# First-layer activations split for two blocks per instruction, out of a pair of PSUM banks

## The chip, the cores and the metric

The kernel runs on one core of one Trainium2 chip. The metric is the device time of one execution in microseconds (us), as the median over timed runs. A program on one core has one span, that of its instructions; the execution's time is a little longer than the span.

## What is computed

The reference is a depthwise causal convolution over the sequence (7 taps, softmaxed weights, one set for each of 8 heads) and, on its result, a mixture of 8 experts. A greedy pass over all sorted gate logits gives every token to exactly one expert, at most 3584 tokens each; each expert is a two-layer network with 1024 hidden units and no bias.

```python
def _attn_ref(x, weight):                 # x: 8 x 3584 x 192, weight: 8 x 7
    ...
    w = w / (np.sum(w, axis=-1, keepdims=True) + 1e-09)
    ...
    out = np.einsum('hk,bskhg->bshg', w, x_unf)

def _moe_ref(x, w_gate, w1, w2):          # x: 28672 x 192, w1: 8 x 192 x 1024, w2: 8 x 1024 x 192
    ...
    for idx in order:
        tok, e = (int(idx) // E, int(idx) % E)
        if assigned[tok] >= 0 or counts[e] >= cap:
            continue
        assigned[tok] = e
        counts[e] += 1
    ...
    for e in range(E):
        mask = assigned == e
        h = np.maximum(x[mask] @ w1[e], 0.0)
        out[mask] = h @ w2[e]
```

## The kernel before

The program has two stages that overlap a little. For the first 155 us the convolution runs as matmuls with Toeplitz matrices (tiles `cv`), with the gate logits (`pl`, `pt`) behind it. Then comes the expert stage, class `FFN`: 56 tiles of 512 tokens, one after the other, and beside them the rest of the routing (which token goes to which expert), cut into small steps that are strewn between the matmuls.

**A tile of the expert stage.** `FFN.run` (from line 1445) goes over the tiles `i` and in each over 8 steps `f`. One step issues, in this order: `l1(i, f)`, a chance for routing steps (`self.bg()`), a piece of the preparation of tile `i + 1` (`prep`), half of the second layer of tile `i - 1` (`l2`, 8 matmuls, with another `self.bg()` inside), after odd steps the store of a finished output block (`store`), routing again, and a piece of the next expert's weights (`wsplit`). "Tile 3, step 1" below is `i = 3, f = 1`. There is no second layer beside tile 0, as there is no tile before it.

**The first layer.** `l1` (line 1320) computes block `f`: 128 of the 1024 hidden units for 512 tokens. Numbers are kept as a high and a low part, so one block is five matmuls of 512 columns into one PSUM bank `ph`. ScalarE then writes the high part `hh` (a Relu that rounds), and VectorE the low part `hl`, which is max(ph, 0) minus `hh`. `hl` needs `ph` and `hh`; the bank `ph` is free when `hl` is done. `l2` multiplies `hh` and `hl` with the second layer's weights, one tile later.

**PSUM.** Eight banks of 512 fp32 a partition. In the expert stage they are: two for `bg` (pool `bgp`, which all routing matmuls and the last gate logits take in turn), two for `y` (second layer), one for `px` and three for `ph`.

**Preparation.** For tiles 1 to 7 the tokens are transposed on TensorE: `transp` (line 1297) writes four blocks into `px` at step 1 (upper 128 features) and again at step 4 (lower 64). At the next step `evac` takes the high part on ScalarE and the low part on VectorE (`xa`, `xd`). Later tiles are transposed on VectorE or by DMA (`shuffle`, `turn`) and use no `px`. Tile 0 is prepared ahead of the expert stage, in `bg` banks.

**The order of the work.** Each engine executes its own instructions in the order in which the program issues them, and waits on semaphores. Routing steps are issued by a planner: class `Pace` keeps an estimated clock for TensorE, VectorE and ScalarE, to which every instruction adds an estimate by its size (class `Meter`: VectorE 0.15 us plus a term in the number of elements, ScalarE 0.22 us plus such a term). `Steps.hook` issues the next routing step unless VectorE's estimated clock is too far ahead of TensorE's (1.8 us in the expert stage) or ScalarE's (3 us). So what an instruction of `l1` is estimated at also moves the routing steps behind it.

A pool hands out any of its buffers that is free when a tile is asked for. A buffer stays taken until the last instruction that reads its tile, wherever that one stands in the order; the first write of the next tile in it waits for that reader.

Of the kernel before, what the change touches and what calls it, by code (L numbers as in the profile page):

```python
# [6 lines left out]
F32 = mybir.dt.float32  # L7
# [3 lines left out]
AF = mybir.ActivationFunctionType  # L11
OP = mybir.AluOpType
AX = mybir.AxisListType
PSUM = bass.MemoryType.PSUM
# [100 lines left out]
def build(ctx, tc, nc, x, weight, wg, attn, LT, wk):  # L115
# [115 lines left out]
    def logits_t(i):  # L231
# [5 lines left out]
        A.activation(o, v, AF.Copy)  # L237

    k.load, k.conv, k.transp, k.logits, k.logits_t = load, conv, transp, logits, logits_t
    k.toeplitz, k.gate_ops = toeplitz, gate_ops  # L240
    return k
# [909 lines left out]
class FFN:  # L1151
# [145 lines left out]
    def transp(self, i, u, bank=None):  # L1297

        x = self.XG[i]
        p = self.px = bank or self.pt.tile([128, 512], F32, name="px")  # L1300
        for b in range(4):
            q = slice(128 * b, 128 * b + 128)
            if u == 0:
                self.nc.tensor.transpose(p[:, q], x[:, b, 0:128], self.ident)
            else:
                self.nc.tensor.transpose(p[0:64, q], x[:, b, 128:D], self.ident)
        if u:
            self.XG.pop(i)
# [11 lines left out]
    def l1(self, i, key, f):  # L1320
        nc = self.nc
        if f == 0:
            self.H[i] = (self.hp[i % 2].tile([128, 8, 512], FR, name="hh"),
                         self.hp[i % 2].tile([128, 8, 512], FR, name="hl"))
        hh, hl = self.H[i]
        ah, al, dh, dl = self.wt(key)[0:4]
        xa, xd = self.XT[i]
        xh, xl = xa[:, 0], xa[:, 1]
        p = self.ph.tile([128, 512], F32, name="ph")
        s = slice(128 * f, 128 * f + 128)  # L1330
        for n, (wt, xx) in enumerate(((ah, xh), (al, xh), (ah, xl), (dh, xd), (dl, xd))):
            nc.tensor.matmul(p, wt[:, s], xx, start=(n == 0), stop=(n == 4))
            if n == 2:
                self.bg()
        nc.scalar.activation(hh[:, f], p, AF.Relu)
        nc.dve = max(nc.dve, nc.act)
        nc.vector.scalar_tensor_tensor(hl[:, f], p, 0.0, hh[:, f].bitcast(F32), op0=OP.max, op1=OP.subtract)

    def l2(self, i, key, b, half):
        nc = self.nc  # L1340
# [143 lines left out]
def moe_kernel(ctx, tc, x, weight, wg, w1, w2, out):  # L1484
    nc = Pace(tc.nc)
# [5 lines left out]
    with ExitStack() as cw:  # L1491
        pool = lambda c, name, bufs, **kw: c.enter_context(tc.tile_pool(name=name, bufs=bufs, **kw))
        late = dict(reuse_waits="tile")
        right = dict(side="right")
# [5 lines left out]
        r = Route(tc, nc, LT, lst, wk, drm)  # L1500
        r.oh_pool = oh
        r.bg = lambda: bgp.tile([128, 512], F32, name="bg")
        ff = FFN(tc, nc, attn, w1, w2, out, r.ident, wr, drm)
# [140 lines left out]
            k.conv(i, mid)  # L1644
        for c in cx[1], cx[2], cx[3], cc:
            c.close()
        ff.pt = pool(cw, "pt", 1, space=PSUM, **right, **late)
        ff.ph = pool(cw, "ph", 3, space=PSUM, **right, **late)
        bg.drain(3)
        nc.lat, nc.las = (0.8, 1.2)  # L1650
        if not got:
# [81 lines left out]
```

## Time and profile before

| what | value |
|---|---|
| median of 3 timed runs | 1236.66 us (1236.03 to 1237.11) |
| the profiled execution | 1234.62 us |
| its span | 1232.9 us |
| mean granted TensorE clock | 0.998 of full speed |
| first `ph` matmul, last one's start | 155.6 us, 1214.8 us |
| `ph` and `y` matmuls | 2240 and 3584 |
| last `bg` output read | 735.8 us |

The profile is one execution, taken by the hardware profiler. PE is TensorE's matmuls and PEld its weight loads, DVE is VectorE, ACT ScalarE, POOL GpSimd, SP the engine whose queue issues most DMAs. A row of the timeline gives start, duration, engine, line, operation, output and inputs, shapes, count, and in brackets the idle time of that engine just before and what ended it. All arithmetic stands on line 56, a helper, so rows are told apart by the names of their tiles. Matmuls are pipelined: their rows overlap, so the distance of starts is what one costs, not its duration.

### The profile page before, as it was taken

Reading aid. Unit: us, or ns where it says so; the run is one execution under the profiler, and the core shown is the slowest. Engines: PE = TensorE matmul, PEld = TensorE weight load, DVE = VectorE, ACT = ScalarE, POOL = GpSimd, SP = SyncE. Lnnn points to the kernel's source line nnn. Section 1 sums busy time; section 2 is a strip of 40 time slices with the busy share of each in tenths; the row PEclk is TensorE's granted clock in tenths of the full one; section 3 lists DMA queues with packets and bytes.
Section 4 is the critical chain, followed back from the end, with each engine's and each line's share of the span. In section 5 each row is a group of like instructions: output and inputs, shape, how many; then the busy total and the mean of one; then the engine's idle time right before and its main releaser. Section 6 shows DMA issues by size and latency. Waiting matters only on the chain.

```text
span 1232.9 us, 21779 instructions
## 1 busy us (share of the span) xinstructions
PE 1201.0 (97%) x7694; PEld 1034.1 (84%) x7694; DVE 983.1 (80%) x2117; ACT 565.6 (46%) x1252; POOL 540.3 (44%) x528
## 2 busy tenths in 40 slices
PE   4999999999999999999999999999999999999997
PEld 2445678899989988889888889999999999999997
DVE  7398789898998988899979866777777777777762
ACT  4454565556445455454554443333433343334332
POOL 3000344444546555545455435444444544543422
PEclk9999999999999999999999999999999999999999
DMA  9999674659427474655343432114323232423100
GB/s 239 347 344 326 230 223 123 176 158 312 153 59 220 133 246 129 219 159 190 88 132 114 116 106 74 49 40 152 108 91 105 97 107 89 159 72 120 49 24 28
DMA packets 129221, 182.03 MB, mean 148 GB/s; under 512 B 21632, under 2 KB 91728, under 8 KB 127440
## 3 DMA queue, kind: packets, MB, share of 16 engines
q1 hardware_dynamic: 86496, 104.15, 27.3%
q0 software_dynamic: 21504, 44.07, 12.0%
q10 hardware_dynamic: 21104, 32.34, 7.8%
q8 instruction: 62, 1.02, 0.4%
q14 instruction: 55, 0.45, 0.1%
HBM read 102.38 MB, written 78.12 MB: 146 GB/s over the span
## 4 chain that ended last, share of the span: by engine, by line
PE 91%; DVE 4%; DMA 2%; ACT 1%; issue 1%; POOL 0%; SPq 0%; ACTq 0%; POOLq 0%; DVEq 0%
PE ph L56 42%; PE y L56 41%; PE cv L56 3%; PE bg L56 3%; DMA X<-in_x_dram 1%; DVE aT L56 1%; PE pl L56 1%; DMA wgr<-in_moe_w_gate_dram 1%; DVE X L56 1%; PE px L56 0%; ACT a L56 0%; ACT X L56 0%; POOL c_mu L173 0%; SPq L194 0%; DVE hl L56 0%
## 5 line engine op out<-in xcount | busy, mean ns | idle before, releaser
L56 PE MATMUL y<-w,hh 128*128 128x384 f32 x1792 | 535.8, 355 | 0.0
L56 ACT ACTIVATE hh<-ph 128x512 fp32r<-128x512 f32 x448 | 268.0, 598 | 470.8 <-PE ph L56 467.9
L56 PE MATMUL y<-w,hl 128*128 128x192 f32 x1792 | 449.0, 251 | 0.0
L56 DVE SCALAR_TENSOR_TENSOR hl<-ph,hh 128x512 fp32r<-128x512 f32 x448 | 307.9, 687 | 133.3 <-ACT hh L56 127.4
L56 PE MATMUL ph<-xa,w 128*128 128x512 f32 x1344 | 395.0, 402 | 0.0
L56 PEld LDWEIGHTS y<-w,hl 128*128 128x128 f32 x1792 | 340.9, 190 | 16.3
L56 PEld LDWEIGHTS y<-w,hh 128*128 128x128 f32 x1792 | 336.3, 188 | 19.8 <-issue 1.7
L1367 POOL DMA_INDIRECT out_dram<-yo,ia x128 | 145.4, 1136 | 211.5 <-DVE yo L56 180.6
L56 PEld LDWEIGHTS ph<-xa,w 128*128 128x128 f32 x1344 | 218.4, 189 | 20.3 <-issue 1.2
L1367 POOL DMA_INDIRECT out_dram<-yo,ib x96 | 96.0, 1000 | 220.0 <-DVE yo L56 212.6
L56 PE MATMUL ph<-xd,w 128*128 128x512 f32 x448 | 177.7, 397 | 1.2 <-DVE xd L56 1.2
L56 PE MATMUL ph<-xd,dl 128*128 128x512 f32 x448 | 174.2, 389 | 0.3 <-DVE dl L56 0.3
L56 DVE STREAM_TRANSPOSE xs<-xg 32x128 f32<-32x128 f32 (+2 forms) x408 | 164.8, 404 | 6.6
L1292 POOL DMA_INDIRECT xg<-attn,ja x128 | 140.6, 1098 | 46.2 <-issue 40.7
L56 ACT ACTIVATE yt<-y 128x192 f32<-128x192 f32 x224 | 73.2, 327 | 94.3 <-PE y L56 91.7
L56 PE MATMUL cv<-X,TH 118*128 118x384 f32 x256 | 99.5, 517 | 17.3 <-DVE TH L56 12.7
L1292 POOL DMA_INDIRECT xg<-attn,jb x96 | 103.5, 1078 | 29.3 <-issue 29.0
L56 DVE TENSOR_TENSOR yo<-y,yt 128x192 f32<-128x192 f32 x224 | 79.3, 354 | 42.8 <-ACT yt L56 40.2
L56 PEld LDWEIGHTS ph<-xd,w 128*128 128x128 f32 x448 | 84.0, 188 | 21.5 <-DVE xd L56 1.7
L56 PEld LDWEIGHTS ph<-xd,dl 128*128 128x128 f32 x448 | 84.2, 188 | 19.9 <-issue 0.5
L56 PEld LDWEIGHTS cv<-X,TH 118*128 118x128 f32 x256 | 45.1, 195 | 47.7 <-issue 12.5
L56 ACT ACTIVATE a<-cv 128x384 f32<-128x384 f32 x128 | 59.2, 493 | 47.4 <-PE cv L56 23.0
(238 smaller groups left out, 918.0 us busy)
## 6 DMA issues: line engine op xcount, KB each, us to landing
attn<-a ACTq DMA_DIRECT2D x16, 1344.0 KB, 10.2
X<-in_x_dram SPq DMA_DIRECT2D x17, 672.0 KB, 14.3
raw<-in_moe_w_dram SPq DMA_DIRECT2D x56, 192.0 KB, 4.0
X<-in_x_dram ACTq DMA_DIRECT2D x15, 672.0 KB, 10.5
kw<-w SPq DMA_DIRECT2D x36, 256.0 KB, 4.3
kv<-w SPq DMA_DIRECT2D x24, 384.0 KB, 5.7
scr<-xs SPq DMA_DIRECT2D x96, 96.0 KB, 2.6
w<-kw SPq DMA_DIRECT2D x6, 1536.0 KB, 7.2
```

Of the source, the lines that this page charges most:

```text
L56: return f(*a, **k)
L1292: self.nc.gpsimd.indirect_dma_start(out=t[:, b], out_offset=None, in_=self.attn[0:rows], in_offset=bass.IndirectOffsetOnAxis(ap=idx[b], ax ...
L1367: st = self.nc.gpsimd.indirect_dma_start(out=self.out, out_offset=bass.IndirectOffsetOnAxis(ap=idx, axis=0), in_=o, in_offset=None, bounds ...
```

## The change

`l1` takes one `ph` tile of two banks for two neighbouring blocks. It issues nothing on ScalarE and VectorE after an even block; after an odd one a single activation and a single VectorE instruction handle both, 1024 elements a partition each. In the last tile every block is still handled alone. The pool `ph` has two such pairs (four banks) instead of three single banks, and `px` loses its own bank: `transp` takes a `bg` buffer.

```diff
@@ class FFN, transp
-        p = self.px = bank or self.pt.tile([128, 512], F32, name="px")
+        p = self.px = bank or self.bank()
@@ class FFN, l1
-        p = self.ph.tile([128, 512], F32, name="ph")
+        if f % 2 == 0:
+            self.pair = self.ph.tile([128, 2, 512], F32, name="ph")
+        p = self.pair[:, f % 2]
...
-        nc.scalar.activation(hh[:, f], p, AF.Relu)
+        if i == len(self.tiles) - 1:
+            c, p = slice(f, f + 1), self.pair[:, f % 2:f % 2 + 1]
+        elif f % 2:
+            c, p = slice(f - 1, f + 1), self.pair
+        else:
+            return
+        nc.scalar.activation(hh[:, c], p, AF.Relu)
         nc.dve = max(nc.dve, nc.act)
-        nc.vector.scalar_tensor_tensor(hl[:, f], p, 0.0, hh[:, f].bitcast(F32), op0=OP.max, op1=OP.subtract)
+        nc.vector.scalar_tensor_tensor(hl[:, c], p, 0.0, hh[:, c].bitcast(F32), op0=OP.max, op1=OP.subtract)
@@ moe_kernel
-        ff.pt = pool(cw, "pt", 1, space=PSUM, **right, **late)
-        ff.ph = pool(cw, "ph", 3, space=PSUM, **right, **late)
+        ff.bank = r.bg
+        ff.ph = pool(cw, "ph", 2, space=PSUM, **right, **late)
```

The rows below are the instructions in the order in which one engine executes them, with the semaphores that one waits for in brackets; the number behind a tile's name tells tiles of one name apart.

First place: ScalarE in tile 0, steps 1 to 3, before. `bg_1883` holds transposed logits, `bg_1887` the next batch of logits, `px_1869` the transposed tokens of tile 1.

```order
L56 ACTIVATE hh_1818<-ph_1850 128x512 [waits PE_49]
L56 ACTIVATE w2_1845<-raw_1561 128x2x192 [waits DMAHW2_49]
L56 ACTIVATE LT_75<-bg_1883 128x8x16 [waits PE_49]
L56 ACTIVATE hh_1818<-ph_1879 128x512 [waits PE_49]
L56 ACTIVATE xa_1908<-px_1869 128x512
L56 ACTIVATE L_1920<-bg_1887 128x4x16 [waits PE_49]
```

The same place of the changed kernel; the tokens are now in `bg_1863`, the two logit tiles in `bg_1877` and `bg_1881`.

```order
L56 ACTIVATE hh_1815<-ph_1817 128x1024 [waits PE_49,Pool_49]
L56 ACTIVATE w2_1840<-raw_1561 128x2x192 [waits DMAHW2_49]
L56 ACTIVATE LT_75<-bg_1877 128x8x16 [waits PE_49]
L56 ACTIVATE xa_1900<-bg_1863 128x512
L56 ACTIVATE L_1912<-bg_1881 128x4x16 [waits PE_49]
```

What moved: one `hh` of 1024 stands where two of 512 stood, and three tiles of the two-buffer pool are read one after the other. TensorE writes them in the order 1863, 1877, 1881:

```order
L56 MATMUL bg_1863<-ident_79,xg_1577 128x128 [waits DMASW7_49]
L56 MATMUL ph_1873<-xa_1747,w1_1548 128x512 x3
L56 MATMUL bg_1877<-ident_79,L_1856 128x128 [waits PE_49,Activation_49]
L56 MATMUL bg_1881<-aT_1773,c_mu_142 32x128 [waits DVE_49,Activation_49]
L56 MATMUL bg_1881<-aT_1773,c_mu_142 32x128 [waits DVE_49] x3
```

Before, the fourth of these rows named other semaphores:

```order
L56 MATMUL px_1869<-ident_79,xg_1577 128x128 [waits DMASW7_49]
L56 MATMUL ph_1879<-xa_1750,w1_1548 128x512 x3
L56 MATMUL bg_1883<-ident_79,L_1862 128x128 [waits PE_49,Activation_49]
L56 MATMUL bg_1887<-aT_1776,c_mu_142 32x128 [waits DVE_49,PE_49]
L56 MATMUL bg_1887<-aT_1776,c_mu_142 32x128 [waits DVE_49] x3
```

The first write of `bg_1881` now waits for ScalarE too: while `bg_1863` is unread it can only have the buffer of `bg_1877`.

Second place: VectorE in tile 0 from step 3 on, before (`w1`, `w2`, `dl` are weight splits, `M1`, `m_f`, `F` routing).

```order
L56 SCALAR_TENSOR_TENSOR hl_1819<-ph_1927,hh_1818 128x512 [waits Activation_49]
L56 TENSOR_REDUCE M1_76<-LT_75 128x16 [waits Activation_49]
L56 TENSOR_TENSOR w2_1845<-raw_1676,w2_1845 128x2x192 [waits DMAHW5_49,Activation_49]
L56 SCALAR_TENSOR_TENSOR hl_1819<-ph_1955,hh_1818 128x512 [waits Activation_49]
L56 SCALAR_TENSOR_TENSOR m_f_1963<-M1_76,Ts_77 128x128 [waits DVE_49]
L56 TENSOR_TENSOR F_1004<-LT_75,m_f_1963 128x4x128 [waits DVE_49]
L56 TENSOR_TENSOR w1_1971<-raw_1848,w1_1971 128x512 [waits DMAHW6_49,DMAHW7_49,DMAHW4_49,Activation_49]
L56 SCALAR_TENSOR_TENSOR hl_1819<-ph_1976,hh_1818 128x512 [waits Activation_49]
L56 TENSOR_TENSOR xd_1909<-px_1966,xd_1909 64x512 [waits PE_49,Activation_49]
L56 TENSOR_TENSOR dl_1803<-raw_1876,w1_1971 64x512 [waits DMAHW0_49,Activation_49]
```

And in the changed kernel:

```order
L56 SCALAR_TENSOR_TENSOR hl_1816<-ph_1873,hh_1815 128x1024 [waits Activation_49]
L56 TENSOR_REDUCE M1_76<-LT_75 128x16 [waits Activation_49]
L56 TENSOR_TENSOR w2_1840<-raw_1676,w2_1840 128x2x192 [waits DMAHW5_49,Activation_49]
L56 SCALAR_TENSOR_TENSOR m_f_1952<-M1_76,Ts_77 128x128 [waits DVE_49]
L56 TENSOR_TENSOR F_1004<-LT_75,m_f_1952 128x4x128 [waits DVE_49]
L56 TENSOR_TENSOR w1_1960<-raw_1843,w1_1960 128x512 [waits DMAHW6_49,DMAHW7_49,DMAHW4_49,Activation_49]
L56 SCALAR_TENSOR_TENSOR hl_1816<-ph_1946,hh_1815 128x1024 [waits Activation_49]
L56 TENSOR_TENSOR xd_1901<-bg_1955,xd_1901 64x512 [waits Activation_49]
L56 TENSOR_TENSOR dl_1800<-raw_1870,w1_1960 64x512 [waits DMAHW0_49,Activation_49]
```

The low parts of blocks 2 and 3 (`ph_1873`) and of 4 and 5 (`ph_1946`) are one instruction each, and that of block 4 moved behind `m_f`, `F` and `w1`.

Third place: ScalarE in tile 3, steps 1 and 2, where routing sorts with 32 matmuls into two `bg` tiles, one for each 16, and ScalarE takes them out into `X1`. Before:

```order
L56 ACTIVATE hh_2607<-ph_2636 128x512 [waits PE_49]
L56 ACTIVATE X1_2404<-bg_2653 128x512 [waits PE_49]
L56 ACTIVATE X1_2404<-bg_2671 128x512 [waits PE_49]
L56 ACTIVATE yt_2700<-y_2617 128x192 [waits DVE_49,PE_49]
L56 ACTIVATE w2_2628<-raw_2500 128x2x192 [waits DMAHW3_49]
L56 ACTIVATE hh_2607<-ph_2709 128x512 [waits PE_49]
L56 ACTIVATE xa_2719<-px_2644 128x512
```

Changed:

```order
L56 ACTIVATE hh_2566<-ph_2568 128x1024 [waits PE_49]
L56 ACTIVATE yt_2615<-y_2576 128x192 [waits DVE_49,PE_49]
L56 ACTIVATE X1_2382<-bg_2619 128x512 [waits PE_49]
L56 ACTIVATE X1_2382<-bg_2637 128x512 [waits PE_49]
L56 ACTIVATE w2_2587<-raw_2464 128x2x192 [waits DMAHW3_49]
L56 ACTIVATE xa_2675<-bg_2602 128x512
```

The tokens (`bg_2602`) were written before both sort tiles and are read after them, so `bg_2619` and `bg_2637` share the one buffer that is left. At steps 4 and 5 of tile 3 the same happens with `X2` and the lower features. The sort of tile 2 and the last one of tile 3 lie between two preparations and have both buffers.

## The prediction

> **What bounds the kernel now.** I read the page first.
>
> ```profile
> span 1232.9 us, 21779 instructions
> PE 1201.0 (97%) x7694; PEld 1034.1 (84%) x7694; DVE 983.1 (80%) x2117; ACT 565.6 (46%) x1252; POOL 540.3 (44%) x528
> L56 ACT ACTIVATE hh<-ph 128x512 fp32r<-128x512 f32 x448 | 268.0, 598 | 470.8 <-PE ph L56 467.9
> L56 DVE SCALAR_TENSOR_TENSOR hl<-ph,hh 128x512 fp32r<-128x512 f32 x448 | 307.9, 687 | 133.3 <-ACT hh L56 127.4
> ```
>
> TensorE is busy 97% of the span. ScalarE stands idle 468 us for `ph`, VectorE 127 us for `hh`: the two engines that the change relieves wait for TensorE, not the other way round. Whether that holds all through, the view by stretches tells (stretch, its length, then busy us of PE, PEld, DVE, ACT, POOL with counts; granted clock, DMA share, GB/s).
>
> ```profile
> 0.00:60.00 60.00, 42.70 (x271) 22.00 (x271) 34.70 (x86) 28.29 (x70) 13.21 (x45) 0.97 1.03 291
> 120.00:180.00 60.00, 56.84 (x545) 39.77 (x543) 45.09 (x85) 36.37 (x86) 25.25 (x24) 1.00 0.75 241
> 540.00:600.00 60.00, 60.00 (x345) 54.21 (x344) 55.02 (x110) 34.57 (x90) 34.34 (x31) 1.00 0.57 179
> 900.00:1000.00 100.00, 100.00 (x570) 90.75 (x569) 75.67 (x160) 38.77 (x78) 46.92 (x45) 1.00 0.30 104
> ```
>
> From tile 2 on TensorE has no gap to speak of, neither beside routing (540 to 600) nor after it (900 to 1000). Last, the waits of TensorE from 150 us to the end, which are what a faster drain of `ph` could still give back.
>
> ```profile
> PE ph L56 <- DVE xd L56: 1.2, 1, 1.2
> PE bg L56 <- DVE r_cc L56: 0.6, 1, 0.6
> PE ph L56 <- DVE dl L56: 0.3, 1, 0.3
> PE bg L56 <- ACT X L56: 0.2, 1, 0.2
> ```
>
> That is 2.3 us in all, and the first, 1.2 us ahead of the first `ph`, lies before anything that the change touches. So there is about **1.1 us to win**, and any new wait of TensorE is paid in full, since it has no slack behind it.
>
> **The cost of one pair.** Nothing of before makes `hh` or `hl` for 1024 elements, but both engines execute instructions of that width.
>
> ```profile
> L56 ACT ACTIVATE X<-bg 128x1024 bf16<-128x1024 bf16 x2 | 1.9, 1021 | 0.6 <-PE bg L56 0.6
> L56 DVE TENSOR_TENSOR LT<-LT,c_mu 128x1024 f32<-128x1024 f32 x2 | 2.4, 1222 | 0.0
> ```
>
> ScalarE: 1.02 us by this row (two banks out of PSUM), at most 2 x 0.598 = 1.20. VectorE: 1.22 by the second row, at most 2 x 0.687 = 1.37. I take 1.02 and 1.22. 55 tiles make 220 pairs: ScalarE saves 220 x (1.196 - 1.021) = 38 us, VectorE 220 x (1.374 - 1.222) = 33 us of work, all of it beside a TensorE that does not wait: **0 us** on the path. What changes for TensorE is when banks and operands come free: a pair is done 1.02 + 1.22 = 2.24 us after its odd block instead of 0.60 + 0.69 = 1.29 us, so about 0.95 us later.
>
> **The undisturbed tile** (tiles 30 to 54). Here is one odd block and its drain.
>
> ```profile
> 861.67 0.88 PE L56 MATMUL ph<-xa,w 128*128 128x512 f32 x3
> 863.03 0.60 ACT L56 ACTIVATE hh<-ph 128x512 fp32r<-128x512 f32 x1 [1.69 <-PE ph L56]
> 863.67 0.69 DVE L56 SCALAR_TENSOR_TENSOR hl<-ph,hh 128x512 fp32r<-128x512 f32 x1 [0.48 <-ACT hh L56]
> 863.95 0.88 PE L56 MATMUL ph<-xa,w 128*128 128x512 f32 x3
> ```
>
> A step takes 863.95 - 861.67 = 2.28 us. As a pair, the drain would end at 863.03 + 2.24 + 0.04 for the handover = 865.3. The banks are wanted three steps after 861.67, at 868.5: 3.2 us to spare. For steps 6 and 7 the second layer wants `hl` in the middle of step 1 of the next tile, some 2.7 us after the drain. So 0 us for 25 tiles, and the last tile drains block by block as before.
>
> **Tile 0 and its border to tile 1: +1.9 us.** Without a second layer the steps are 1.2 us long, and ScalarE and VectorE are full. The rows of before:
>
> ```profile
> 161.26 0.39 PE L56 MATMUL ph<-xd,dl 128*128 128x512 f32 x1
> 162.19 0.51 ACT L56 ACTIVATE w<-raw 128x384 fp32r<-128x384 f32 x1
> 162.84 0.65 PE L56 MATMUL bg<-aT,c_mu 128*32 128x128 f32 x16
> 162.94 0.28 ACT L56 ACTIVATE LT<-bg 128x128 f32<-128x128 f32 x1 [0.24 <-PE bg L56]
> 166.12 0.40 PE L56 MATMUL ph<-xd,dl 128*128 128x512 f32 x1
> 167.80 0.36 DVE L56 TENSOR_REDUCE M<-LT 128x16 f32<-128x128 f32 x1
> 168.08 0.55 DVE L56 TENSOR_TENSOR w<-raw,w 128x384 fp32r<-128x384 f32 x1
> 169.00 0.39 PE L56 MATMUL ph<-xd,dl 128*128 128x512 f32 x1
> 169.15 0.34 DVE L56 SCALAR_TENSOR_TENSOR m_f<-M,Ts 128x128 f32<-128x128 f32 x1
> 169.52 0.69 DVE L56 TENSOR_TENSOR F<-LT,m_f 128x512 bf16<-128x512 f32 x1
> 170.13 0.68 DVE L56 TENSOR_TENSOR w<-raw,w 128x512 fp32r<-128x512 f32 x1
> 171.45 0.68 DVE L56 TENSOR_TENSOR xd<-px,xd 64x512 fp32r<-64x512 f32 x1
> 171.50 0.94 PE L56 MATMUL ph<-xa,w 128*128 128x512 f32 x3
> 172.16 0.69 DVE L56 TENSOR_TENSOR dl<-raw,w 64x512 fp32r<-64x512 f32 x1
> 173.00 0.47 PE L56 MATMUL ph<-xd,dl 128*128 128x512 f32 x1 [0.25 <-DVE dl L56]
> ```
>
> Two waits arise. First, at step 2 the new logits (162.84) must wait for the buffer of the transposed ones, as the tokens hold the other. ScalarE takes those out (`LT`) only after the pair 0/1: block 1 ends at 161.65, `hh` 161.69 to 162.71, `w` 0.51 to 163.23, `LT` 0.28 to 163.52. The logits start at 163.57 instead of 162.84: 0.73 us late.
>
> Second, tile 1's first block needs the banks of blocks 4/5. Block 5 ends at 169.39 + 0.73 = 170.12, its `hh` at 171.18. VectorE: block 3 ends at 166.52 + 0.73, its pair's `hh` at 168.31, so `hl` of 2/3 ends at 169.57. Behind it stand, with the rows' durations, the reduction 0.36, `w` 0.55, `m_f` 0.34, `F` 0.69 and `w` 0.68, to 172.2, then the pair 4/5 to 173.4, `xd` to 174.1 and `dl` to 174.8. So TensorE's `ph` of 171.50, due at 172.23, starts at 173.4, and its row of 173.00, which waits for that `dl`, moves to 174.9: **+1.9**, which contains the 0.73. Behind it the pair 6/7 (`w` 0.68, then 1.22) is there at 176.7, 1.8 us ahead of the second layer's use. Bounds: 0.7, if the VectorE chain closes up by the 1.2 us, and 3.0, if the pair costs 1.37 and `w` comes late too.
>
> **Tile 3, two sorts in one buffer: +1.6 us.** The two rows of each place in before:
>
> ```profile
> 218.63 1.20 PE L56 MATMUL bg<-oa,X 128*32 128x128 bf16 x32
> 219.39 1.09 ACT L56 ACTIVATE X<-bg 128x512 bf16<-128x512 f32 x2 [1.05 <-PE bg L56]
> 227.37 1.19 PE L56 MATMUL bg<-oa,X 128*32 128x128 bf16 x32
> 228.12 1.08 ACT L56 ACTIVATE X<-bg 128x512 bf16<-128x512 f32 x2 [1.04 <-PE bg L56]
> ```
>
> ScalarE starts on the first 16 matmuls' output 0.76 us after TensorE began, takes half of 1.09, and only then may matmul 17 write: 0.76 + 0.58 + 0.04 = 1.38 us after the start instead of 0.60. That is 0.78 us twice, **1.6 us**. ScalarE was idle ahead of both (1.05 and 1.04), so it can hardly be later than that; nothing below 1.2 seems possible and 2.4 is the upper end, if `yt`, which now stands ahead of `X`, delays the first. The other preparations (tiles 2, 4 to 7, and tile 1 itself) meet no second routing tile between writing and reading: 0.
>
> **The planner.** An even block no longer charges VectorE's estimate, and a pair saves it 0.15 us, so routing runs ahead: its last matmuls move from tile 29, step 4 to tile 28, step 2. Nothing waits for its end but the tokens of tile 32, which are fetched in tile 30: 0 us, and 0.6 either way for the one routing wait of before (`r_cc`).
>
> **Sum.** 1.9 + 1.6 = +3.5 us on the profiled execution's 1234.62 (span 1232.9 and 1.7 us around it), 1238.1. The median of the runs shown is 1236.66, 2.0 above that execution, so the same sum gives **1240.2**.
>
> **Rivals.** *Not slower.* The relieved VectorE closes up: its 33 us of saved work lie mostly in the stretch where it is 55 of 60 us busy, the waits for `r_cc` and `dl` go, and tile 0 loses only 0.7. Then +0.7 + 1.2 - 0.9 = +1.0, 1237.7; without the sort's waits, were a buffer free in time, -0.2, 1236.5. It decides if VectorE's chain at 169 to 173 us ends under 0.5 us later than before. For it: each pair has one start-up less. Against: in tile 0 VectorE would stand idle for the pair's `hh`, work it had before. [...]
>
> *Late pairs all along the routing.* Where VectorE has a backlog the drain comes close to the next use:
>
> ```profile
> 739.41 0.68 DVE L56 SCALAR_TENSOR_TENSOR hl<-ph,hh 128x512 fp32r<-128x512 f32 x1
> 740.47 0.88 PE L56 MATMUL ph<-xa,w 128*128 128x512 f32 x3
> ```
>
> This `hl` ends at 740.09 and its bank is wanted at 740.47. With 1.22 for 0.68 it would be 0.16 late. If ten such places (of some 110 pairs beside routing) are late by half a us, 5 us more: 1245.2. Against: the planner counts the pair's cost ahead of the next routing step.
>
> *The clock falls.* The rows show 0.97 for the first 60 us, where TensorE idles 17 us, and 1.00 for 120 to 180, where it idles 3. Lost there: 0.03 x 60 = 1.8 us; as much again would give 1242.0. [...] The trace's 1.00 beside 3 us of gaps speaks against it.
>
> *The change doesn't do what it says*: the rows of order show the pairs in place, so this gets nothing.
>
> **How the numbers follow.** A measurement of this kernel can tell about 0.2%, 2.5 us. Forecast (+2.5 to +5.5): 0.60. Late pairs: 0.10. Clock: 0.02, also slower. Not slower: 0.28, of which 0.24 within 0.2%, and 0.04 faster by more (0.01 of it for the whole 33 us). Slower 0.72, same 0.24, faster 0.04. The range leaves out the lower end of the second and the worst of the third: 1237.2 to 1245.0.
>
> **What would show it.** Right: TensorE's waits from 150 us on list `ph` or its `dl` at 173 to 175 us for over 1 us, and twice 0.8 us ahead of a `bg<-oa,X` in tile 3; `hh` x220 near 1020 ns, `hl` x220 near 1220; the time from tile 30 to the end unchanged. Wrong: less than 0.7 us of new waits ahead of 176 us; new waits between tiles 4 and 29 that add up to over 1 us; another step than 2.28 us in the second half.

## The result and the profile after

The changed kernel takes 1243.12 us (median of 6 runs, 1242.02 to 1246.31), the kernel before 1236.53 us beside it (6 runs, 1235.63 to 1237.29). The ratio is 1.0054, 95% interval 1.0043 to 1.0065: slower by 6.6 us, where +3.5 was forecast. The profiled run has a span of 1241.4 us.

The page of the changed kernel:

```profile
span 1241.4 us, 21397 instructions
PE 1203.8 (97%) x7694; PEld 1034.9 (83%) x7694; DVE 944.6 (76%) x1897; ACT 531.8 (43%) x1032; POOL 532.4 (43%) x528
L56 ACT ACTIVATE hh<-ph 128x1024 fp32r<-128x1024 f32 (+1 forms) x228 | 230.5, 1011 | 554.4 <-PE ph L56 554.2
L56 DVE SCALAR_TENSOR_TENSOR hl<-ph,hh 128x1024 fp32r<-128x1024 f32 (+1 forms) x228 | 274.4, 1203 | 203.0 <-ACT hh L56 202.4
```

The relief is there and is worth nothing. The `hh` rows fell from 268.0 to 230.5 us and the `hl` rows from 307.9 to 274.4. The idle time ahead of the same instructions grew by more than what was saved: from 470.8 to 554.4 us on ScalarE and from 133.3 to 203.0 us on VectorE. The stretch after routing shows it again (columns as in the same view of before: length, busy us of PE, PEld, DVE, ACT, POOL, clock, DMA share, GB/s):

```profile
900.00:1000.00 100.00, 100.00 (x570) 90.72 (x569) 73.71 (x146) 35.36 (x56) 43.26 (x42) 1.00 0.27 93
```

TensorE is full as before, with as many matmuls (570) in 100 us. So the loss is not spread out. The waits of TensorE from 150 us on (sum, times, longest) say where to look:

```profile
PE ph L56 <- DVE hl L56: 2.7, 6, 0.8
PE bg L56 <- ACT X L56: 1.6, 3, 0.7
PE ph L56 <- DVE xd L56: 0.8, 1, 0.8
PE bg L56 <- ACT LT L56: 0.5, 1, 0.5
PE ph L56 <- DVE dl L56: 0.2, 1, 0.2
PE bg L56 <- DVE xd L56: 0.2, 1, 0.2
```

Before there was no wait for `hl` and 0.2 us for `X`. The wait for `LT` is in tile 0, and so is the `hl` that the first block of tile 1 waits for:

```profile
165.10 0.65 PE L56 MATMUL bg<-aT,c_mu 128*32 128x128 f32 x16 [0.50 <-ACT LT L56]
173.36 1.22 DVE L56 SCALAR_TENSOR_TENSOR hl<-ph,hh 128x1024 fp32r<-128x1024 f32 x1
174.63 0.98 PE L56 MATMUL ph<-xa,w 128*128 128x512 f32 x3 [0.71 <-DVE hl L56]
```

To place the losses, I took the start of each tile's first `ph` matmul and the end of the last `y` matmul from the timelines, counted from the start of tile 0's first `ph`. "Later" is the changed kernel minus the kernel before.

| place | before, us | after, us | later by |
|---|---|---|---|
| tile 0 | 155.62 | 157.69 | 0 (set) |
| tile 1 | 171.50 | 174.63 | 1.05 |
| tile 3 | 214.08 | 217.29 | 1.13 |
| tile 4 | 237.35 | 242.73 | 3.31 |
| tile 7 | 295.56 | 300.97 | 3.33 |
| tile 8 | 313.86 | 320.25 | 4.32 |
| tile 30 | 740.47 | 746.66 | 4.12 |
| tile 55 (last) | 1197.80 | 1203.99 | 4.12 |
| end of last `y` | 1225.36 | 1233.75 | 6.32 |

Four places make up 6.22 of the 6.32 us: tile 0 (1.05), tile 3 (2.18), tiles 7 to 30 (0.79), the last tile (2.20). Between tiles 30 and 55 nothing is lost. Ahead of tile 30, routing's matmuls stand earlier, so that tile 27 starts 11.6 us later than before; that excess is gone at tile 30 and is no loss.

The start of tile 0 is 2.07 us later in this profile. Most of that is scatter: three profiles of the kernel before put it at 155.62, 159.11 and 159.77 us, those of changed kernels anywhere from 155.72 to 162.30. But 0.38 us of it belongs to the change, and the zero of the table hides it. In the nine profiles of kernels that put tile 1's tokens into `bg`, the weight load of the first `ph` waits 0.4 us for ScalarE to read an output of the convolution (`a`), and that `ph` starts 1.07 us after the last `cv` matmul. In the four with a bank for `px` in tile 0 (before, e5, e8, e9) there is no such wait, and it starts 0.68 us after. Probably `ph` now begins in a bank that the convolution still uses; no run tests that. The same block then waits for `xd` in all of them, and the late start only shortens that wait. The row of before, then the wait of the weight load and the row of the changed kernel:

```profile
157.78 0.50 PE L56 MATMUL ph<-xd,w 128*128 128x512 f32 x1 [1.22 <-DVE xd L56]
```

```profile
PEld ph L56 <- ACT a L56: 0.4, 1, 0.4
159.47 0.50 PE L56 MATMUL ph<-xd,w 128*128 128x512 f32 x1 [0.82 <-DVE xd L56]
```

Counted from this `xd` matmul, tile 0 costs 1.43 us instead of 1.05, and the whole 6.70 instead of 6.32, which is close to the 6.6 us between the medians. Most of what is left to the 8.5 us between the spans is the scatter ahead of tile 0.

### The profile page after: what moved, and what is told of

Same layout as the page of the kernel before. It is cut to its first block, busy times and chain, and to the rows that moved or that the text cites. A ratio compares the mean times of both kernels' runs of the same rounds, so it can differ in the third digit from the quotient of the medians.

```text
span 1241.4 us, 21397 instructions
## 1 busy us (share of the span) xinstructions
PE 1203.8 (97%) x7694; PEld 1034.9 (83%) x7694; DVE 944.6 (76%) x1897; ACT 531.8 (43%) x1032; POOL 532.4 (43%) x528
## 3 DMA queue, kind: packets, MB, share of 16 engines
q8 instruction: 62, 1.02, 0.4%
## 4 chain that ended last, share of the span: by engine, by line
PE 87%; DMA 5%; DVE 4%; ACT 2%; issue 1%; SPq 1%; POOL 0%; ACTq 0%; POOLq 0%; DVEq 0%
PE ph L56 41%; PE y L56 39%; PE bg L56 4%; DMA X<-in_x_dram 3%; PE cv L56 3%; PE pl L56 1%; DMA wgr<-in_moe_w_gate_dram 1%; DVE aT L56 1%; DVE X L56 1%; DVE hl L56 1%; DMA xs<-scr 1%; ACT hh L56 0%; ACT X L56 0%; ACT a L56 0%; DVE xd L56 0%
## 5 line engine op out<-in xcount | busy, mean ns | idle before, releaser
L56 ACT ACTIVATE hh<-ph 128x1024 fp32r<-128x1024 f32 (+1 forms) x228 | 230.5, 1011 | 554.4 <-PE ph L56 554.2
L56 DVE SCALAR_TENSOR_TENSOR hl<-ph,hh 128x1024 fp32r<-128x1024 f32 (+1 forms) x228 | 274.4, 1203 | 203.0 <-ACT hh L56 202.4
L1375 POOL DMA_INDIRECT out_dram<-yo,ia x128 | 139.0, 1086 | 232.3 <-DVE yo L56 193.9
L1375 POOL DMA_INDIRECT out_dram<-yo,ib x96 | 100.2, 1043 | 223.3 <-DVE yo L56 215.9
L1292 POOL DMA_INDIRECT xg<-attn,ja x128 | 143.6, 1122 | 47.1 <-issue 40.8
L1292 POOL DMA_INDIRECT xg<-attn,jb x96 | 97.3, 1013 | 29.3 <-issue 29.3
L56 ACT ACTIVATE yt<-y 128x192 f32<-128x192 f32 x224 | 73.1, 326 | 29.8 <-PE y L56 15.2
```

The lines of the kernel that those rows point to most:

```text
L56: return f(*a, **k)
L1292: self.nc.gpsimd.indirect_dma_start(out=t[:, b], out_offset=None, in_=self.attn[0:rows], in_offset=bass.IndirectOffsetOnAxis(ap=idx[b], ax ...
L1375: st = self.nc.gpsimd.indirect_dma_start(out=self.out, out_offset=bass.IndirectOffsetOnAxis(ap=idx, axis=0), in_=o, in_offset=None, bounds ...
```

## The experiments

### The last tile

The prediction gave the last tile 0 us, since it "drains block by block as before". The timeline shows it waiting (brackets: idle time before, and what ended it):

```profile
1203.99 0.88 PE L56 MATMUL ph<-xa,w 128*128 128x512 f32 x3
1205.36 0.60 ACT L56 ACTIVATE hh<-ph 128x512 fp32r<-128x512 f32 x1 [0.78 <-PE ph L56]
1205.99 0.69 DVE L56 SCALAR_TENSOR_TENSOR hl<-ph,hh 128x512 fp32r<-128x512 f32 x1 [0.37 <-ACT hh L56]
1206.74 0.96 PE L56 MATMUL ph<-xa,w 128*128 128x512 f32 x3 [0.30 <-DVE hl L56]
1209.12 0.88 PE L56 MATMUL ph<-xa,w 128*128 128x512 f32 x3
```

Block 1 writes the other bank of the pair, yet starts only when `hl` of block 0 (1205.99 + 0.69) is done. Two steps take 1209.12 - 1203.99 = 5.13 us instead of 2 x 2.285 = 4.57: 0.56 us, four times. The order of TensorE's instructions shows that the program itself holds this wait. The first matmul of blocks 5, 6 and 7 of the last tile, in the changed kernel:

```
L56 MATMUL ph<-xa,w_13082 128x512 [waits DVE_49]
L56 MATMUL ph<-xa,w_13082 128x512 [waits PE_49]
L56 MATMUL ph<-xa,w_13082 128x512 [waits DVE_49]
```

Odd blocks wait for VectorE. In a paired tile they wait for nothing, since no reader stands between the two halves: dependencies are kept for the two-bank tile, not for its banks. Whether the other bank could be written without that wait is not shown: no run here left it out while draining one bank alone.

**e1** pairs the last tile too:

```diff
-        if i == len(self.tiles) - 1:
-            c, p = slice(f, f + 1), self.pair[:, f % 2:f % 2 + 1]
-        elif f % 2:
+        if f % 2:
```

> The changed kernel, but the last tile's blocks are drained in pairs like all others. Theory (a block that is drained alone out of a two-bank tile keeps TensorE from writing the tile's other bank until its hl is done: four waits of 0.46 us and a restart each, 2.2 us in the profile of the changed kernel): the last tile takes 2.2 us less, 1243.1 - 2.2 = 1240.9 us. Rival (the loss belongs to the last tile because the second layer behind it waits for late operands): pairing makes it worse, by up to 1 us, 1244.

Measured: 1241.62 us (12 runs), ratio 1.0033 (1.0022 to 1.0045). Tile 55 starts 4.13 us later than before and the end is 4.13 us later: the last tile's 2.2 us are gone. The other tiles start within 0.06 us of where they start in the changed kernel, but for tiles 5 to 7, which are 0.36 us late and make it up at tile 8.

**e3** handles every tile as the last one is handled (`if True:` in place of the condition).

> The changed kernel with every tile treated as its last one: two-bank tiles, but each block drained by itself. Theory of the wait on the tile's other bank: every odd block waits for the hl of the even one, 0.55 us for two steps, a steady tile takes 18.29 + 2.2 = 20.5 us, and 55 more tiles make at least +121 us: 1364 us or more. Rival (the loss is special to the last tile): a steady tile stays at 18.3 us, 1243 us.

Measured: 1400.08 us (one run). A tile in the second half takes 20.50 us instead of 18.29, 2.21 more, which is 4 x 0.55. TensorE's waits, then two blocks:

```profile
PE ph L56 <- DVE hl L56: 100.6, 205, 3.2
...
907.32 0.97 PE L56 MATMUL ph<-xa,w 128*128 128x512 f32 x3 [0.30 <-DVE hl L56]
909.70 0.88 PE L56 MATMUL ph<-xa,w 128*128 128x512 f32 x3
```

Two-bank tiles that are drained bank by bank cost some 160 us; the pair instruction is not only a saving there but what makes such tiles bearable.

### Sharing `bg` without pairs

**e2** is the kernel before with `transp` in a `bg` buffer, as in the change; blocks are single.

```diff
-        p = self.px = bank or self.pt.tile([128, 512], F32, name="px")
+        p = self.px = bank or self.bank()
...
-        ff.pt = pool(cw, "pt", 1, space=PSUM, **right, **late)
+        ff.bank = r.bg
```

> The kernel before, three single ph banks and one instruction for each block, only with the transposed tokens in a bg buffer. Theory (the shared buffers cost 0.8 us at each of two sorts in tile 3 and 0.6 us at step 2 of tile 0): 1236.5 + 2.2 = 1238.7 us, waits of bg matmuls for ACT X of some 1.5 us. Rival (what was lost there belongs to the pairs, whose late drain keeps ScalarE busy): as before, 1236.5 us, no such waits.

Measured: 1239.45 us, ratio 1.0019 (1.0006 to 1.0031). Its two waits for `X` in tile 3, then the three waits of the changed kernel's tile 3:

```profile
222.96 0.70 PE L56 MATMUL bg<-oa,X 128*32 128x128 bf16 x16 [0.69 <-ACT X L56]
232.60 0.69 PE L56 MATMUL bg<-oa,X 128*32 128x128 bf16 x16 [0.70 <-ACT X L56]
```

```profile
223.81 0.70 PE L56 MATMUL bg<-oa,X 128*32 128x128 bf16 x16 [0.69 <-ACT X L56]
232.90 0.69 PE L56 MATMUL bg<-oa,X 128*32 128x128 bf16 x16 [0.70 <-ACT X L56]
238.61 0.70 PE L56 MATMUL bg<-oa,X 128*32 128x128 bf16 x16 [0.17 <-DVE xd L56]
```

Counted like the table, e2's tiles 1 to 3 start as before, and tile 4 is 1.77 us late, as is all the rest (1.88 at the end). So sharing costs 0.9 us at each of the two sorts. In tile 0 the logits do wait for `LT` (0.37 us), which the table's zero hides: counted from the `xd` matmul, tile 1 is 0.44 us late and the end 2.34. So the expectation held, 0.6 + 1.6 = 2.2 us by the sum, with somewhat less in tile 0 and more in tile 3. With the pairs a third sort of tile 3 (steps 5 to 7, 0.35 us) is late as well, its buffer held until `xd` is out, and tile 0 loses 1 us more than in e2 (1.43 against 0.44).

### The pairs beside routing

**e5** has single banks and `px` of its own up to tile 7, pairs from tile 8 on (last tile included).

```diff
+        if i < 8:
+            p = self.ph.tile([128, 512], F32, name="ph")
+        else:
+            ...
+            if i == 8:
+                cp.close()
+                ff.ph = pool(cw, "ph2", 2, space=PSUM, **right, **late)
```

> Tiles 0 to 7 as before (own px bank, three single ph banks), tiles 8 to 55 in pairs, the last one too. Theory (all of the loss sits in tiles 0 to 3 and in the last tile; a pair costs and gives nothing where TensorE is the bound): before plus at most the 0.8 us that the changed kernel loses between tiles 7 and 30, 1236.5 to 1237.3 us, steady tile 18.29 us. Rival 1 (ScalarE's and VectorE's saved work, some 29 and 33 us, is worth something): 1234 us or less. Rival 2 (late pairs beside the routing): 1239 us or more.

Measured: 1241.3 us, ratio 1.0025 (1.0014 to 1.0036): the theory's 1236.5 to 1237.3 us missed, and the time lies where the rival of late pairs has it. Up to tile 7 it runs like before (0.08 us earlier), so nothing ahead of that is at fault. Tile 8 starts 1.75 us late, because its first pair needs the old single banks, whose last `hl` stands behind routing:

```profile
319.07 0.67 DVE L56 SCALAR_TENSOR_TENSOR hl<-ph,hh 128x512 fp32r<-128x512 f32 x1
319.66 0.35 DVE L56 TENSOR_TENSOR yo<-y,yt 128x192 f32<-128x192 f32 x1
319.80 0.97 PE L56 MATMUL ph<-xa,w 128*128 128x512 f32 x3 [1.67 <-DVE hl L56]
```

The handover from single banks to pairs has a part in that, which only e5 has. By tile 10 0.76 us of it is regained (0.99 late); from there to tile 30 another 1.3 us are lost, of which TensorE's waits for routing (`r_cc`) show 0.4. So it showed that the pairs are not free beside routing, and not how much they cost. Tile 8 of the changed kernel, which has no handover, tells more:

```profile
313.14 0.63 ACT L56 ACTIVATE xa<-xs 128x512 fp32r<-128x512 f32 x1 [2.92 <-DMA xs<-scr]
314.54 0.36 DVE L56 TENSOR_TENSOR yo<-y,yt 128x192 f32<-128x192 f32 x1 [3.06 <-ACT yt L56]
...
315.55 0.41 DVE L56 MAX8 r_w<-X 128x8 f32<-128x256 f32 x1
...
318.65 0.43 DVE L56 MAX8 r_w<-X 128x8 f32<-128x256 f32 x1
318.99 1.20 DVE L56 SCALAR_TENSOR_TENSOR hl<-ph,hh 128x1024 fp32r<-128x1024 f32 x1
320.25 0.97 PE L56 MATMUL ph<-xa,w 128*128 128x512 f32 x3 [0.82 <-DVE hl L56]
```

ScalarE waits for a transfer, so VectorE waits 3.06 us for ScalarE, and then has the queue that the planner gave it. `l1` now adds nothing to VectorE's estimate after an even block, so the planner let two rounds of routing (four MAX8, two MATCH_REPLACE8, 2.7 us) in ahead of the pair's `hl`.

**e4** takes that to the test. It is e1, but the planner is charged for each block as in the kernel before:

```diff
+        act = max(nc.act, nc.pe) + 0.22 + 512 / 1370
+        dve = max(nc.dve, nc.pe, act) + 0.15 + 512 / 960
...
+        nc.act, nc.dve = act, dve
```

> The kernel after with the last tile paired too (as in e1), and with one thing more: the planner that deals out the background work charges each 512-wide block as the kernel before did (0.22 + 512/1370 us for ScalarE, 0.15 + 512/960 us for VectorE, at every block), although the instructions are issued in pairs as after. So the background stands at the steps at which before has it. Theory: the 0.8 us that the FFN stage loses between the starts of tiles 7 and 30 comes from the planner's lighter charge, which lets routing into an even step ahead of the pair's hl. Then tile 30 starts 3.3 us later than in before (counted from tile 0's start) instead of 4.1, the wait of 0.8 us for hl at the start of tile 8 is gone, and the time is 0.8 us under that of e1, a ratio of about 1.0027. Rival: it is the length of the pair's instructions themselves that makes tile 8 late. Then the wait stays, tile 30 starts 4.1 us later, and the ratio is that of e1, 1.0033.

**e6** is e4 with routing's `m_f` and `F` of tile 0 behind the last pairs (`TAIL`, last entry 13 to 22):

> The kernel e4 with one number changed: in tile 0 the last entry of the order of the tail moves from step 13 to step 22, so that the m_f of the border and the first piece of routing (about 1 us of VectorE) stand behind the hl of the pairs 4/5 and 6/7 instead of ahead of them. Theory: tile 0 loses 1.05 us because VectorE's chain reaches the hl of the last pair of the tile late, so that the first block of tile 1 finds no free pair of banks: the wait of 0.7 us of ph for hl near the start of tile 1 falls to 0.2 or less and the loss to about 0.35 us. Rival: it is ScalarE's hh, or the wait for LT, that sets it, and VectorE's place in the order does nothing: the loss stays at 1.05 us.

**e8** is the kernel before, beside them:

> The kernel before, unchanged. The start of tile 0 stood at 155.6 us in its first profile and between 157.1 and 159.8 us in those of the changed kernels, although the change doesn't touch what runs before it. Theory: this start varies from run to run with the landing of the loads, so that it may stand anywhere between 155.5 and 160 us here, with the stretch from tile 0's start to the end the same within 0.2 us as in the first profile. Rival: the change delays the conv stage. Then it stands at 155.6 us again, within 0.3.

Measured: e4 1254.32 us (ratio 1.0071, 1.0055 to 1.0087), e6 1251.98 (1.0056, 1.0042 to 1.0071), e8 1243.42. They ran on another chip than e1, e2, e3 and e5, one on which the kernel before has a median of 1245.41 us. e8's tile 0 starts at 159.11 us: that start varies from run to run. But its stretch from there to the end is 1074.91 us, 5.17 more than in the first profile, so this half of its expectation is wrong. TensorE's waits for routing's `r_cc` and `r_v` are 2.2 us in e8 against 0.6, which is a part of it. VectorE and ScalarE of e8, between 156 and 760 us, stand idle for nothing that the profile shows ("issue"); in the first profile the `hl` line reads 1.3 us and the `hh` line is absent:

```profile
DVE hl L56 <- issue: 15.2, 17, 1.9
ACT hh L56 <- issue: 31.7, 32, 2.5
```

So e4 cannot be held against e1, only against e8: tile 8 has no wait for `hl` any more (4.96 us late at tile 7 and at tile 8), but 3.72 us are lost in tile 3 alone, and the end is 7.02 us late. The ratio is far from the 1.0027 expected, so the test is open until the same kernels stand beside each other on one chip (e9 to e12). e6 against e4 is fair, on one chip: in tile 0 the wait of the first row, in e4, is absent in e6, while the other is in both.

```profile
179.90 0.96 PE L56 MATMUL ph<-xa,w 128*128 128x512 f32 x3 [0.73 <-DVE hl L56]
```

```profile
169.44 0.65 PE L56 MATMUL bg<-aT,c_mu 128*32 128x128 f32 x16 [1.12 <-ACT LT L56]
```

Tile 1 starts 0.93 us after that of e8 instead of 1.52. So VectorE's order behind `hl` makes the wait at tile 1's start, as the prediction had it; the rest, more than the 0.35 expected, is the logits' wait for `LT`, which is 1.12 us on this chip and 0.50 in the first profile of the changed kernel.

**e9 to e12** are the kernels before, after, e1 and e4 once more, on a third chip.

> The kernel before, unchanged, so that the three that follow stand beside it on one chip. On the chip of the run before last the stretch from tile 0's start to the end was 5.2 us longer than in the first profile, by waits of TensorE for routing's r_v and r_cc in tiles 19 to 29. Theory: how long routing's results take to come differs between chips, so the changed kernels are to be compared with this run alone. No further time is forecast: the stretch may stand anywhere between that of the first profile (1069.7 us) and 5.5 us above it.

> The kernel after, unchanged, on the same chip as e9. Theory: the losses of tiles 0 and 3 and of the last tile are the program's own, so that against e9 tile 1 starts 1.0 to 1.2 us later (counted from tile 0's start), tile 4 3.2 to 3.4 us, and the last tile takes 2.2 us longer than in e9, on any chip. Rival: they hang on how late the loads and the routing come on a chip, and then tiles 1 and 4 move by over 0.3 us; the last tile's 2.2 us stays in either case.

> The kernel e1 on the same chip as e9 and e10. Theory: 2.2 us under e10, all of it in the last tile, with every other tile as in e10 within 0.1 us.

> The kernel e4 on the same chip as e11, which differs from it in the planner's charge alone. Theory: the wait for hl at the start of tile 8 is that of the planner's lighter charge, so it is in e11 (0.8 us) and not here, and between the starts of tiles 7 and 30 e12 loses 0.8 us less to e9 than e11 does. Rival: charged as before, the planner puts steps at other places where they are late (routing's r_cc, tile 3's X), so that e12 is not faster than e11, though the wait at tile 8 is gone: then it loses as much or more between tiles 8 and 30, and its time is at or above that of e11.

Counted as in the first table:

| later than e9 at | e10 (after) | e11 (e1) | e12 (e4) |
|---|---|---|---|
| tile 1 | 1.08 | 1.14 | 1.16 |
| tile 4 | 3.36 | 3.45 | 3.82 |
| tile 7 | 3.54 | 3.88 | 3.82 |
| tile 8 | 4.39 | 5.46 | 3.82 |
| tile 30 | 4.01 | 5.19 | 3.69 |
| tile 55 | 4.01 | 5.19 | 3.69 |
| end | 6.19 | 5.19 | 3.69 |
| median, us | 1244.06 | 1241.63 | 1240.30 |
| ratio (95%) | 1.0054 (1.0035 to 1.0073) | 1.0040 (1.0026 to 1.0054) | 1.0022 (1.0013 to 1.0031) |

e9's stretch is 1069.79 us, that of the first profile within 0.05. e10 repeats the losses of tiles 0 and 3 and of the last tile (6.19 - 4.01 = 2.18). Tile 8 is where the two readings part. e11 waits for `hl` there, e12 doesn't; VectorE in e12 has `xd` and then `hl`, with no routing between:

```profile
319.31 0.96 PE L56 MATMUL ph<-xa,w 128*128 128x512 f32 x3 [1.42 <-DVE hl L56]
```

```profile
316.56 0.69 DVE L56 TENSOR_TENSOR xd<-xs,xd 64x512 fp32r<-64x512 f32 x1
...
317.28 1.23 DVE L56 SCALAR_TENSOR_TENSOR hl<-ph,hh 128x1024 fp32r<-128x1024 f32 x1
...
320.16 0.88 PE L56 MATMUL ph<-xa,w 128*128 128x512 f32 x3
```

From tile 7 to tile 30 e12 loses nothing (3.82 to 3.69), e10 0.47 and e11 1.31, so that e12 is 1.44 better than e11 there, where 0.8 was expected. So here the planner's lighter charge is the cause, and not the pair's length, which is the same in both. A transfer that comes earlier isn't what spares e12 the wait: ScalarE's wait for it ends 12.19 us after the start of tile 7 there, later than in e10 (12.04), which has the wait. The medians of e11 and e12 are 1.33 us apart and their intervals overlap, so it is this wait, more than the time, that shows the cause; and in tile 3 e12 loses some 0.4 us more than e11. That e11 differs from e10 by up to 1.1 us at tile 8, against its expectation, comes from the transfer ahead of `xa`, which ends ScalarE's wait 12.77 us after the start of tile 7 in e11 and 12.04 us in e10. In all four kernels with the lighter charge (after, e1, e10, e11) tile 8 starts 7.10 to 7.11 us after that, so whatever is late there goes straight into tile 8. On the second chip the gain of e4 was given back: between tiles 8 and 30 it lost 2.06 us to e8, with the charge as before. So the planner's part is shown at tile 8; its sum over the routing depends on the chip.

None of the versions reaches the kernel before: the nearest with pairs is e12, with ratio 1.0022 on its chip.

## Why the prediction was right, and where it was not

- **Slower, by waits of TensorE**: right. It forecast +3.5 us and 1240.2 us, with 1237.2 to 1245.0 as range; measured were +6.6 and 1243.12. The reason given, that TensorE has no slack behind a new wait and the relieved engines wait for it, is what the page shows. That the time lies inside the range is in part luck: 2.99 of the 6.70 us came from two places that the sum put at nothing, and tile 0 cost less than forecast. Of the prediction's own signs of being right, the wait for `ph` at tile 1's start came at 0.71 us instead of over 1, and the time from tile 30 to the end did not stay as it was (+2.20).
- **Cost of a pair**: 1.02 us and 1.22 us by rows of the same width; the pairs' median durations are 1.026 and 1.224 us. (ScalarE's row reads one `bg` buffer of 512 fp32 as 1024 bf16, line 574, not two banks; the 1.026 us is for two.) Saved by groups: 37.5 us of ScalarE (38 forecast) and 33.5 of VectorE (33), worth 0, as forecast. A pair is shorter than two blocks by 0.17 us on ScalarE (1.026 against 2 x 0.598) and by 0.15 us on VectorE (1.224 against 2 x 0.687); the time shows that here, with TensorE busy 97% of the span, this buys nothing.
- **Undisturbed tile**, 0: right. 18.29 us a tile in both kernels.
- **Tile 0 and its border, +1.9**: right place and both waits, mis-sized; 1.43 counted from tile 0's `xd` matmul (1.05 by the table). The logits came 0.57 us late, with a wait of 0.50 for `LT`, and not 0.73. The pair 4/5 ended at 174.58, that is 172.89 on the time axis of before, and not at 173.4; so the border cost 0.87 and not 1.17, and `dl` cost nothing more (0.24 us of wait, 0.25 before). The 1.2 us wait for `xd` that the prediction read as ahead of the first `ph` stands inside tile 0's first block.
- **Tile 3, +1.6**: the mechanism and its two places are shown by e2, at 0.9 instead of 0.78 us each. The third sort, said to have both buffers, cost 0.35 more. In all 2.18, inside the 1.2 to 2.4 given.
- **The planner and the pairs beside routing, 0**: mis-sized by 0.79 us. The step that failed reads "An even block no longer charges VectorE's estimate, and a pair saves it 0.15 us, so routing runs ahead". What stands behind routing on VectorE was left out: the pair's `hl`, and with it the banks of the next tile. That cost 0.99 us at tile 8; 0.74 came back by tile 10, where before waits 0.6 us for `r_cc` and the changed kernel doesn't, and 0.54 more went by tile 30 without a new wait of TensorE above 0.2 us. The rival of late pairs expected such a wait for `hl` behind VectorE's backlog at ten places; it came at one, and by e12 through routing let in ahead of the pair, not through the pair's length, which the rival had as its reason.
- **The last tile, 0**: wrong, and with 2.20 us the largest miss. "Drains block by block as before" took it that a bank comes free by itself. In a two-bank tile of this program it doesn't: the odd block waits for the even block's reader. The order of the instructions could have shown that wait ahead of time.
- **The clock**: 0.997 against 0.998; that rival fell.

## What to carry to other kernels

Merging the drains of two PSUM banks saved 37.5 us of work on ScalarE and 33.5 us on VectorE here; look first whether the matmuls wait for them, and if they don't, ask only what becomes late. In this program a tile of several banks is released as a whole, so any path that still drains it bank by bank waits (0.56 us in two steps of the last tile), and borrowing a buffer of another pool takes away that pool's overlap wherever two writes follow each other (0.9 us at each of two sorts in e2). And where a planner orders work by estimates, moving an instruction moves the charge too: look at what it lets in ahead of the instruction that became later.

## What was not expected of the hardware

e3 shows the granted clock falling after a long wait. Stretches of 4 us (columns as above; the clock is the third number from the end), and the row of TensorE's timeline that ends the wait:

```profile
154.00:158.00 4.00, 3.86 (x19) 2.27 (x17) 2.17 (x4) 2.90 (x7) 3.67 (x4) 1.00 0.66 210
158.00:162.00 4.00, 1.82 (x35) 1.11 (x34) 3.80 (x5) 1.14 (x3) 3.37 (x4) 1.00 1.02 322
162.00:166.00 4.00, 2.93 (x20) 1.77 (x21) 1.48 (x3) 0.20 (x2) 2.00 (x2) 0.62 0.86 284
```

```profile
163.07 1.65 PE L56 MATMUL ph<-xa,w 128*128 128x512 f32 x3 [2.43 <-DVE hl L56]
```

TensorE waited 2.43 us until 163.07, and the stretch in which it went on had a clock of 0.62; three matmuls that take 0.97 us elsewhere took 1.65. Between 900 and 1000 us of the same kernel, with a wait of 0.30 us at every odd block and 94.00 us busy of 100, it was 1.00. In this run the small gaps came without a fall, and a fall followed the long one; whether the wait brought it about, no run here tells.

The other is the difference between chips: the same program, the kernel before, has medians of 1237.5, 1245.4 and 1237.4 us on the three chips of the experiments, and on the slowest ScalarE stood for 31.7 us ahead of `hh` and VectorE for 15.2 us ahead of `hl` without a releaser in the profile. What holds them there stays open.
